# Two-layer attention and expert kernel: state products for two tiles in one run, two more residuals through TensorE, and a new written order

## The chip, the cores and the metric

The kernel runs on one core of a Trainium2 chip. The metric is the device time of one execution in microseconds. A profiled execution also gives a trace of every instruction on TensorE (PE, its weight loads PEld), VectorE (DVE), ScalarE (ACT), GpSimd (POOL) and SyncE (SP, which here only issues DMAs).

## What is computed

2048 tokens of width 576 pass through two layers. Each layer is a linear attention block with a residual, and then a block that picks one of 64 experts per head, with a residual. Cut to what matters:

```python
def _A_ref(x, wqkv, wo):                       # 32 heads of 18
    qkv = (x @ wqkv) ...
    phi = lambda t: jnp.where(t > 0, t + 1, jnp.exp(t)) + 1e-6
    pq, pk = phi(q), phi(k)
    kv = jnp.einsum("bhsd,bhse->bhde", pk, v)
    z = jnp.einsum("bhsd->bhd", pk)
    o = (pq @ kv) / (pq . z + 1e-6)
    return o @ wo
def _B_ref(x, w_q, k1, k2, u, v):              # 32 heads, 8 x 8 experts, one chosen
    q1, q2 = halves of x @ w_q
    s1, s2 = q1 @ k1.T, q2 @ k2.T
    e = argmax(s1) * 8 + argmax(s2)
    return sum over heads of gelu(x . u[e]) * v[e]
x = x + _A_ref(layernorm(x), wqkv, wo)
x = x + _B_ref(layernorm(x), w_q, k1, k2, u, v)   # and both once more
```

The state kv and its sum need all tokens of a layer. So each layer has a part that ends with the state, and a part that starts with it.

## The kernel before

The tokens stand in 16 tiles of 128. Every float32 matrix is split into a high and a low part, and a product of a tile with a 576 wide weight is 28 matmuls in groups of 10, 8 and 10 (high with high, high with low, low with high). These are the groups of lines L236 and L452 in the profile, 10 or 8 matmuls to a row.

The first part of a layer takes each tile through normalizing (yf), turning (by TensorE as ptf, or by a DMA through memory: t_df is written and rf is read back), splitting (thif and tlof), and the products for key, value and query (ppk, ppv, ppq). ScalarE and VectorE make the positive keys and queries (ek, eq) and copy the values into one of two buffers (v, L275). `front_state` (L320) then adds the tile's keys times values to the state kva, one accumulator in PSUM for the whole layer: ten matmuls that write 64 of 128 columns each. PSUM is a pool of four accumulators of 128 x 1024, and all results of TensorE go through it.

In layer 0 another job runs beside this: the experts' keys are multiplied into w_q (`fold_mm`, L618), 16 steps of 8 matmuls each that write 32 columns, from 64 loads of 288 KB on SyncE (fold). The loads land in a ring of ten buffers. Positive queries of layer 0 are stored (pq_d) and read back later.

The second part forms the state's sum and its product with wo (z, m), and takes each tile through the division (o), turning (pto, or t_do and ro), the output product ppo (L452), the residual x (L441, VectorE), normalizing (yb), turning (ptb, or t_db and rb), the scores pps (14 matmuls, L494), a choice of the best expert in code on VectorE for a group of two tiles, which ends with ct (L558), the gelu (g), and the product of both (cg, on GpSimd, L565). `exp_T` turns it on TensorE (pc, L473) and splits it on ScalarE and VectorE (chi, clo, L476 and L478), and `exp_out` multiplies it with the experts' values (po, L585, 4 matmuls, two with chi and two with clo) and adds the residual on VectorE (L441). For some tiles of layer 1 the residual goes another way: `exp_base` (L574) multiplies the tile's x with the identity matrix into the accumulator po first, 2 instructions that the trace shows as 4 records, the output is added to it there, and ScalarE copies the sum out (L590). Before the change these are tiles 10, 11 and 12. The last group of layer 1 is the tiles 8 and 9.

The order of all of it is written out by hand. Each step is a generator cut into pieces at its `yield`s, and a text lists the pieces: `st0.3` is the next piece of the state step of layer 0, tile 3, and `num1.0x2` two pieces of the division of tile 0 in layer 1. `play` runs them one by one, inside `with in_order(PE, ACT, DVE, POOL, SP)`, so every engine, SyncE's queue of DMAs with it, executes its instructions strictly in the order in which the text emits them. An instruction that waits holds back all that stands behind it on its engine. `wu` pieces are matmuls on scratch data at the start (warm_up).

The text's pieces that the change and the prediction touch: st (state), F and wf (fold matmuls and their loads), wk, wv, wq (weights), fl and ln (first tiles), bT (turning before the scores), po and base.

## Time and profile before

| | |
|---|---|
| median of 3 runs | 722.04 us (721.49 to 722.27) |
| profiled execution | 720.1 us |
| its span in the trace | 718.3 us, so 1.8 us lie outside |
| mean granted TensorE clock | 0.992 |
| PE busy | 694.6 us (97%) |
| DVE, ACT, POOL busy | 465.2, 340.0, 232.4 us |
| DMA moved | 131.23 MB, mean 183 GB/s |

In rows of the timeline the first number is the start in microseconds from the span's start, the second the duration from the first start to the last end of the instructions of the row. Then come the engine, the line, the operation, what it writes and reads, the shape, and how many. In square brackets stands the idle time of that engine just before the row, and what ended it. The ends of matmuls are modelled and overlap the next start by a little, so costs of TensorE are best taken from start to start.

The page's 40 slices of the span (busy tenths of TensorE and VectorE, granted TensorE clock, DMA):

```profile
PE   8999999999998999999999999999999999999994
...
DVE  6763713121437788779867857631477798898776
...
PEclk9999999999999999999999999999999999999996
DMA  8799789700128557574786586444568575545302
```

TensorE is the full row; VectorE is nearly full in the stretches around 260 to 400 and 560 to 700 us, where the second parts of the layers run.

### The profile page before, as it was taken

What the parts mean: (1) busy time and instruction counts of PE and PEld (TensorE: products, weight loads), DVE (VectorE), ACT (ScalarE), POOL (GpSimd) and SP (SyncE); (2) the same over time, 40 slices, a digit from 0 to 9 for tenths busy, and PEclk for the clock granted to TensorE, in tenths of its full rate; (3) what the DMA queues carried; (4) which work ended last, traced back from release to release, by engine and by line L of the source; (5) the groups of instructions that cost most, each with busy time, mean ns of one, the idle gap of its engine ahead of it and who ended that gap; (6) DMA issues with size and microseconds to landing.
All of it is one profiled execution on the core that took longest, in us unless ns stands there. A gap on an engine that the chain in (4) does not pass through costs nothing.

```text
span 718.3 us, 14467 instructions
## 1 busy us (share of the span) xinstructions
PE 694.6 (97%) x5292; PEld 640.5 (89%) x5292; DVE 465.2 (65%) x840; ACT 340.0 (47%) x645; POOL 232.4 (32%) x490
## 2 busy tenths in 40 slices
PE   8999999999998999999999999999999999999994
PEld 5998988999996988988999999999999899898873
DVE  6763713121437788779867857631477798898776
ACT  5552422211324446464755575564565645644342
POOL 4231100000032455445642622420135545444242
PEclk9999999999999999999999999999999999999996
DMA  8799789700128557574786586444568575545302
GB/s 268 228 315 321 221 280 291 237 18 1 34 75 251 189 168 238 186 242 133 238 266 214 175 253 199 144 153 103 162 182 243 185 198 177 163 158 182 100 16 99
DMA packets 109276, 131.23 MB, mean 183 GB/s; under 512 B 11926, under 2 KB 69270, under 8 KB 109206
## 3 DMA queue, kind: packets, MB, share of 16 engines
q1 hardware_dynamic: 109206, 130.32, 58.4%
q8 instruction: 41, 0.67, 0.4%
q14 instruction: 29, 0.24, 0.1%
HBM read 80.83 MB, written 49.45 MB: 181 GB/s over the span
## 4 chain that ended last, share of the span: by engine, by line
PE 51%; DVE 14%; issue 13%; DMA 10%; POOL 5%; ACT 3%; SPq 3%; POOLq 0%; DVEq 0%; ACTq 0%
PE ppk L236 10%; PE ppq L236 9%; PE ppv L236 9%; PE pps L494 8%; PE ppo L452 6%; DMA ro<-t_do 2%; PE fold_ps L618 2%; PE po L585 2%; SPq L218 2%; PE kva L320 2%; DVE x L441 1%; DVE m L527 1%; DMA rf<-t_df 1%; POOL o L418 1%; DMA whi<-hl_d 1%
## 5 line engine op out<-in xcount | busy, mean ns | idle before, releaser
L236 PE MATMUL ppk<-whi,thif 128*128 128x288 f32 x320 | 49.9, 300 | 2.8 <-ACT thif L224 1.4
L226 DVE TENSOR_TENSOR tlof<-rf,thif 128x640 fp32r<-128x640 f32 x27 | 22.2, 826 | 45.8 <-ACT thif L224 13.3
L452 PE MATMUL ppo<-ohi,thio 126*128 126x288 f32 (+1 forms) x320 | 49.9, 298 | 0.2
L236 PEld LDWEIGHTS ppk<-whi,thif 128*128 128x128 f32 x320 | 44.4, 188 | 5.6 <-ACT thif L224 1.9
L236 PE MATMUL ppk<-whi,tlof 128*128 128x288 f32 x320 | 48.4, 295 | 0.0
L236 PE MATMUL ppv<-whi,thif 128*128 128x252 f32 x320 | 48.2, 296 | 0.0
L236 PE MATMUL ppv<-whi,tlof 128*128 128x252 f32 x320 | 47.9, 295 | 0.0
L452 PEld LDWEIGHTS ppo<-ohi,thio 126*128 126x128 f32 (+1 forms) x320 | 44.5, 189 | 1.6 <-ACT thio L224 0.5
L236 PEld LDWEIGHTS ppv<-whi,thif 128*128 128x128 f32 x320 | 44.6, 189 | 0.7 <-DVE ek L252 0.2
L236 PEld LDWEIGHTS ppv<-whi,tlof 128*128 128x128 f32 x320 | 44.9, 189 | 0.0
L494 PE MATMUL pps<-shi,thib 128*128 128x512 f32 x160 | 43.4, 401 | 1.3 <-DVE x L441 0.8
L236 PEld LDWEIGHTS ppk<-whi,tlof 128*128 128x128 f32 x320 | 44.5, 188 | 0.0
L494 PE MATMUL pps<-shi,tlob 128*128 128x512 f32 x160 | 42.5, 395 | 0.6 <-DVE tlob L226 0.6
L275 ACT ACTIVATE v<-ppv 128x252 f32<-128x252 f32 x64 | 20.8, 379 | 45.9 <-PE ppv L236 27.7
L236 PE MATMUL ppk<-wlo,thif 128*128 128x288 f32 x256 | 39.8, 296 | 0.8 <-POOL wlo L131 0.8
L452 PE MATMUL ppo<-ohi,tloo 126*128 126x288 f32 x256 | 40.3, 295 | 0.1
L252 DVE SCALAR_TENSOR_TENSOR ek<-ppk,ek 128x576 f32<-128x576 f32 x32 | 24.2, 756 | 24.7 <-ACT ek L246 23.3
L452 PE MATMUL ppo<-olo,thio 126*128 126x288 f32 x256 | 40.1, 295 | 0.0
L236 PE MATMUL ppv<-wlo,thif 128*128 128x252 f32 (+1 forms) x256 | 39.3, 295 | 0.0
L170 ACT ACTIVATE yb<-x,mb 128x576 f32<-128x576 f32 x32 | 24.8, 774 | 30.5 <-POOL mb L167 27.8
L236 PE MATMUL ppq<-whi 128*128 128x288 f32 x260 | 39.0, 298 | 0.0
L184 ACT ACTIVATE yb<-x,rsb 128x640 f32<-128x640 f32 x32 | 29.4, 920 | 18.6 <-POOL rsb L175 17.8
(175 smaller groups left out, 1685.7 us busy)
## 6 DMA issues: line engine op xcount, KB each, us to landing
fold<-in_wq_t SPq DMA_DIRECT2D x64, 288.0 KB
t_df<-qf SPq DMA_DIRECT2D x27, 320.0 KB
rf<-t_df SPq DMA_DIRECT2D x108, 80.0 KB
t_do<-qo SPq DMA_DIRECT2D x27, 320.0 KB
ro<-t_do SPq DMA_DIRECT2D x108, 80.0 KB
whi<-hl_d SPq DMA_DIRECT2D x26, 320.0 KB
t_db<-qb SPq DMA_DIRECT2D x25, 320.0 KB
rb<-t_db SPq DMA_DIRECT2D x100, 80.0 KB
```

The lines of the kernel that those rows point to most:

```text
L170: nc.scalar.activation(y.rearrange("p a b -> p (a b)")[:, :D], xt, AF.Square, bias=m[:, 0:1], accum_out=m[:, 1:2])
L184: nc.scalar.activation(y, x2, AF.Identity, scale=rs[:, 0:1], bias=rs[:, 1:2])
L218: nc.sync.dma_start(r[32 * a:32 * a + 32].rearrange("r (i e) -> r i e", i=4), t_d[kind, t][:, a * w:(a + 1) * w].rearrange("(i r) e -> r i ...
L226: (nc.gpsimd if (who or kind, l) in LO_POOL or (who or kind, l, t) in LO_POOL else nc.vector).tensor_tensor(l4, src, h.bitcast(F32), op=AL ...
L236: nc.tensor.matmul(o[:, at:at + c1 - c0], tt[a == "lo"][:, b, :], wb[:, cols + c0:cols + c1], start=(i == 0), stop=(i == len(todo) - 1))
L252: nc.vector.scalar_tensor_tensor(e2, halves(p), 0.0, e2, op0=ALU.max, op1=ALU.add)
L275: nc.scalar.activation(vt[:, c:c + 2].rearrange("p c h e -> p (c h) e")[:, :, :63], x.rearrange("p (c e) -> p c e", c=4), AF.Copy)
L320: nc.tensor.matmul(a[64 * h:64 * h + 64, c * 72:c * 72 + n], vt[:, c, h], fk[:, k0:k0 + n], start=(t == 0 and c == 0), stop=(t == NT - 1), ...
L452: nc.tensor.matmul(p[:, h * 512:h * 512 + HALF], hl[a][:r, b], w[:r, h * HALF:(h + 1) * HALF], start=(i == 0), stop=(i == len(todo) - 1))
L494: nc.tensor.matmul(p[:, :512], hl[a == "lo"][:, b, :], shi[:, b] if w == "hi" else slo[:, blocks(REM)[b][1]], start=(i == 0), stop=(i == l ...
L585: nc.tensor.matmul(p[:, b * 512:b * 512 + HALF], c[i], vmix[:, b * HALF:(b + 1) * HALF], start=(i == 0 and not based), stop=(i == 1))
L618: nc.tensor.matmul(p[32 * j:32 * j + 32, at:at + c1 - c0], kpad[:, ch // 2, 24 - 8 * a:56 - 8 * a], st[:, c0:c1], start=(a == 0), stop=(a ...
```

## The change

`front_state` is called for every odd tile and does the ten matmuls of the tile before and of its own in one run; the accumulator of a layer's state is taken at tile 1, not 0. The score step is written a little differently, with the same instructions. Tiles 8 and 9 of layer 1 get their residuals through `exp_base` too (the set BASE is not read by the code; the pieces `base1.8` and `base1.9` in the text are what counts). The text is new from end to end. Warm-up matmuls are 29 and were 27.

```diff
-BASE = {10, 11, 12}
+BASE = {10, 11, 12, 8, 9}
...
     def front_state(l, t):
-        fk, vt = tt.pop(("fk", l, t)), v5[t % 2]
-        if t == 0:
+        if t == 1:
             kva[l] = psum(f"kva{l}")
         a = kva[l]
-
-        for c in range(NB):
-            for h in range(2):
-                k0, n = (c * HC + 54 * h, 72) if c < 4 else (4 * HC + 36 * h, 36)
-                nc.tensor.matmul(a[64 * h:64 * h + 64, c * 72:c * 72 + n], vt[:, c, h], fk[:, k0:k0 + n],
-                                 start=(t == 0 and c == 0), stop=(t == NT - 1), skip_group_check=True)
-
+        for u in (t - 1, t):
+            fk, vt = tt.pop(("fk", l, u)), v5[u % 2]
+            for c in range(NB):
+                for h in range(2):
+                    k0, n = (c * HC + 54 * h, 72) if c < 4 else (4 * HC + 36 * h, 36)
+                    nc.tensor.matmul(a[64 * h:64 * h + 64, c * 72:c * 72 + n], vt[:, c, h], fk[:, k0:k0 + n],
+                                     start=(u == 0 and c == 0), stop=(u == NT - 1), skip_group_check=True)
...
-            po1.12 po1.11 po1.12 po1.11 sel1.8 po1.12 sel1.8 gel1.8 sel1.8x2 po1.15x2 cT1.8x3 po1.8 po1.9 po1.8x2 po1.9x2
...
+            po1.11x2 sel1.8x5 po1.15x2 cT1.8x3 po1.9x3 po1.8x3
```

In the rows of the order below, a name's last number only tells buffers apart and the number before it is the tile.

**State runs, TensorE, first part of layer 1 (near 398 us in the trace before).** Before:

```order
L473 MATMUL pc_8_5081<-ident,cg_8_5069 128x128 x2
L320 MATMUL kva_3742<-ek_5_4778,v_1_87 64x72 x8
L320 MATMUL kva_3742<-ek_5_4778,v_1_87 64x36 x2
L320 MATMUL kva_3742<-ek_6_4926,v_0_86 64x72 x8
L320 MATMUL kva_3742<-ek_6_4926,v_0_86 64x36 x2
L585 MATMUL po_8_5114<-vmix,chi_8_5110 128x288 x2
L585 MATMUL po_8_5114<-vmix,clo_8_5111 128x288 x2
```

Now:

```order
L472 MATMUL pc_8_5069<-ident,cg_8_5060 128x128 x2
L320 MATMUL kva_4145<-ek_4_4617,v_0_86 64x72 x8
L320 MATMUL kva_4145<-ek_4_4617,v_0_86 64x36 x2
L320 MATMUL kva_4145<-ek_5_4803,v_1_87 64x72 x8
L320 MATMUL kva_4145<-ek_5_4803,v_1_87 64x36 x2
L583 MATMUL po_8_5111<-vmix,chi_8_5092 128x288 x2
L583 MATMUL po_8_5111<-vmix,clo_8_5093 128x288 x2
```

The run had the keys ek of tiles 5 and 6 and now has those of 4 and 5; tile 6's value product stands just ahead in both. Tile 4's own run, which stood alone elsewhere, is gone. Over both layers the state's 320 matmuls stood in 21 runs (12 of them of a single tile, one of four) and now stand in 16, each of two tiles.

**Normalizing of tile 0 in layer 1, ScalarE (near 560 us).** yb is made in two steps (L170, L184); thib_2 is a high part that comes back by DMA. Before:

```order
L244 ACTIVATE eq_4_7091<-ppq_4_7062 128x576
L245 ACTIVATE eq_4_7091<-eq_4_7091 128x576
L246 ACTIVATE eq_4_7091<-eq_4_7091,small 128x576
L224 ACTIVATE thib_2_7125<-rb_2_7015 128x640
L170 ACTIVATE yb_0_7168,mb_0_7157<-x_0_6996,mb_0_7157 128x576
L184 ACTIVATE yb_0_7168<-x_0_6996,rsb_0_7174 128x640
L170 ACTIVATE yb_1_7190,mb_1_7185<-x_1_7171,mb_1_7185 128x576
L200 ACTIVATE thib_0_7223<-ptb_0_7194 128x640
```

Now:

```order
L170 ACTIVATE yb_0_7091,mb_0_7001<-x_0_6998,mb_0_7001 128x576
L244 ACTIVATE eq_4_7093<-ppq_4_7062 128x576
L245 ACTIVATE eq_4_7093<-eq_4_7093 128x576
L246 ACTIVATE eq_4_7093<-eq_4_7093,small 128x576
L184 ACTIVATE yb_0_7091<-x_0_6998,rsb_0_7097 128x640
L224 ACTIVATE thib_2_7144<-rb_2_7057 128x640
L170 ACTIVATE yb_1_7153,mb_1_7151<-x_1_7141,mb_1_7151 128x576
L200 ACTIVATE thib_0_7192<-ptb_0_7135 128x640
```

Both of tile 0's steps moved ahead of thib_2, the first also ahead of query tile 4's finish. On TensorE the turning of tile 0 (ptb_0) moved from behind the output product of tile 13 to ahead of it.

**The end, TensorE.** po with x and ident is `exp_base`. Before:

```order
L473 MATMUL pc_11_8940<-ident,cg_11_8937 128x128 x2
L585 MATMUL po_11_8735<-vmix,chi_11_8947 128x288 x2
L585 MATMUL po_11_8735<-vmix,clo_11_8948 128x288 x2
L585 MATMUL po_12_8931<-vmix,chi_11_8947 128x288 x2
L585 MATMUL po_12_8931<-vmix,clo_11_8948 128x288 x2
L473 MATMUL pc_8_8991<-ident,cg_8_8985 128x128 x2
L585 MATMUL po_8_8998<-vmix,chi_8_8994 128x288 x2
L585 MATMUL po_8_8998<-vmix,clo_8_8995 128x288 x2
L585 MATMUL po_9_9003<-vmix,chi_8_8994 128x288 x2
L585 MATMUL po_9_9003<-vmix,clo_8_8995 128x288 x2
```

Now:

```order
L472 MATMUL pc_11_8938<-ident,cg_11_8934 128x128 x2
L583 MATMUL po_12_8921<-vmix,chi_11_8943 128x288 x2
L583 MATMUL po_12_8921<-vmix,clo_11_8944 128x288 x2
L572 MATMUL po_11_8960<-x_11_8513,ident 128x288 x2
L583 MATMUL po_11_8960<-vmix,chi_11_8943 128x288 x2
L583 MATMUL po_11_8960<-vmix,clo_11_8944 128x288 x2
L572 MATMUL po_8_8970<-x_8_8795,ident 128x288 x2
L472 MATMUL pc_8_8999<-ident,cg_8_8993 128x128 x2
L583 MATMUL po_9_8724<-vmix,chi_8_9002 128x288 x2
L583 MATMUL po_9_8724<-vmix,clo_8_9003 128x288 x2
L583 MATMUL po_8_8970<-vmix,chi_8_9002 128x288 x2
L583 MATMUL po_8_8970<-vmix,clo_8_9003 128x288 x2
```

Tile 11's identity product (before: earlier, behind the scores of tile 11) comes behind tile 12's output, and tile 8's ahead of the last pc; tile 9's took the place that tile 11's had. On VectorE the two residuals behind the last clo are gone, and on ScalarE two copies stand last.

Elsewhere: the 16 fold steps stand in 11 runs on TensorE and stood in 9. At the start, SyncE asks for the weight blocks 0, 1, 3, 2, 4 and for tile 2 between the last two, where it asked for 1, 0, 2, 3, 4 and tile 2 later; ScalarE rounds weight block 0 ahead of scaling tile 0, and GpSimd's small key step stands ahead of the first tile's statistics. Behind the first query products the value product of tile 2 stands where the key product of tile 2 stood. On SyncE the load for the last part of fold step 9 stands behind the store of query tile 3 and the four loads of tile 13's turned rows.

188 lines of the change are left out of this document (88 added, 100 removed).

## The prediction

> **What bounds the kernel now.** I read the busy line first, then windows of it, then TensorE's timeline for what ended each of its waits.
>
> ```profile
> PE 694.6 (97%) x5292; PEld 640.5 (89%) x5292; DVE 465.2 (65%) x840; ACT 340.0 (47%) x645; POOL 232.4 (32%) x490
> ```
>
> TensorE is busy for 694.6 of 718.3 us, and no other engine that computes is above 65%. So a new order can win in two ways only: TensorE's work gets shorter, or the 718.3 - 694.6 = 23.7 us in which it is not busy get fewer. The windows say where those are (columns: window, its length, then busy time and instructions of PE, PEld, DVE, ACT and POOL, then granted clock, DMA share and GB/s).
>
> ```profile
> 0.00:40.00 40.00, 35.42 (x253) 29.16 (x254) 29.26 (x59) 23.61 (x38) 15.62 (x41) 1.00 0.82 245
> 40.00:204.00 164.00, 164.00 (x1461) 155.46 (x1460) 57.62 (x108) 45.83 (x104) 9.10 (x23) 1.00 0.57 183
> 204.00:240.00 36.00, 34.17 (x312) 27.95 (x311) 20.57 (x40) 15.06 (x34) 12.08 (x24) 1.00 0.65 200
> ...
> 560.00:680.00 120.00, 117.33 (x744) 107.10 (x743) 103.97 (x191) 62.05 (x111) 57.42 (x114) 1.00 0.57 170
> ...
> 706.00:718.30 12.30, 3.12 (x12) 2.23 (x10) 6.05 (x16) 1.58 (x4) 1.13 (x2) 0.51 0.32 120
> ```
>
> The head lacks 4.6 us, the turn to the first output products 1.8, the last 12.3 us lack 9.2: together 15.6 of the 23.7. From 40 to 204 TensorE never stops; there only its own work counts. In 560 to 680 VectorE is busy for 104 of 120 us, so an order that makes VectorE late costs TensorE there.
>
> **The change part by part.** Durations are those of the profiled execution (720.1 us, span 718.3). The runs' median, 722.04, is 1.94 above it, and the sum is applied to both. A difference under 0.2%, 1.44 us, can't be told from none.
>
> *State products, two tiles in one run.* Each state run (kva, L320) writes 64-column pieces, and the products on both sides of it pay for the turn. TensorE's timeline (start, duration, engine, line, operation) has a run of two tiles and one of a single tile between like neighbours:
>
> ```profile
> 169.99 1.50 PE L236 MATMUL ppv<-whi,tlof 128*128 128x252 f32 x10
> 171.42 1.43 PE L320 MATMUL kva<-ek,v 128*64 128x72 f32 x40
> ...
> 174.25 1.22 PE L236 MATMUL ppk<-wlo,thif 128*128 128x288 f32 x8
> ...
> 176.64 1.50 PE L236 MATMUL ppk<-whi,thif 128*128 128x288 f32 x10
> 177.98 1.23 PE L236 MATMUL ppk<-wlo,thif 128*128 128x288 f32 x8
> 179.05 1.49 PE L236 MATMUL ppk<-whi,tlof 128*128 128x288 f32 x10
> 180.47 0.81 PE L320 MATMUL kva<-ek,v 128*64 128x72 f32 x20
> ...
> 182.63 1.23 PE L236 MATMUL ppk<-wlo,thif 128*128 128x288 f32 x8
> ```
>
> An undisturbed group of ten product matmuls takes 177.98 - 176.64 = 1.34 us. From 169.99 to 174.25 lie one such group, the run of two tiles, and one more group: the run costs 4.26 - 2.68 = 1.58. From 179.05 to 182.63 it is one tile between two groups: 3.58 - 2.68 = 0.90. Joining two singles is worth 2 x 0.90 - 1.58 = 0.22 us. The order of TensorE has 21 state runs before and 16 now: 5 x 0.22 = **-1.1 us**. Nothing hides it, as these runs stand where TensorE doesn't stop. Bounds: -0.6 (half of the joins had another disturbance beside them) and -1.4. The pair also adds a wait: there are two value buffers, so ScalarE can't copy the values of the pair's successor until the pair's run is through, and the key finishes queued behind that copy on ScalarE wait with it. As TensorE has a whole product (3.8 us from 176.64 to 180.47) between a pair and the next use of what these copies free, I count 0; where that cover is missing it costs about the 0.7 to 1.3 of the waits that end on ScalarE in the fences below.
>
> *Fold products* (32-column pieces, L618): the same 128 instructions, in 11 runs instead of 9. Rows of TensorE, and of SyncE's issues (SPq) in the same stretch:
>
> ```profile
> 54.98 2.19 PE L618 MATMUL fold_ps<-fold,kpad 128*32 128x320 f32 x32
> 57.10 1.60 PE L236 MATMUL ppk<-whi,thif 128*128 128x288 f32 x10
> 58.53 1.23 PE L236 MATMUL ppk<-wlo,thif 128*128 128x288 f32 x8
> ...
> 96.29 1.50 PE L236 MATMUL ppq<-whi,tlof 128*128 128x288 f32 x10
> ...
> 112.57 2.36 PE L618 MATMUL fold_ps<-fold,kpad 128*32 128x320 f32 x32
> ...
> 222.23 2.63 PE L618 MATMUL fold_ps<-fold,kpad 128*32 128x320 f32 x16
> ...
> 99.90 0.33 SPq L284 DMA_DIRECT2D pq_d<-eq  x1
> ...
> 108.32 2.47 SPq L218 DMA_DIRECT2D rf<-t_df  x4
> ```
>
> The group behind a run takes 58.53 - 57.10 = 1.43 instead of 1.34, and the run's start costs about as much: 0.1 to 0.25 us a run, two more runs, **+0.3**. A run can also wait inside for its loads: 2.36 instead of 2.19 at 112.57, and at 222.23 16 records took longer than 32. In the new order the last load for the fourth run of this kind (fold tile 9) stands on SyncE behind the store of query tile 3 and four loads of a turned tile. That store is issued 99.90 - (96.29 + 1.34) = 2.3 us after its product ends, the four loads take 2.5, and 288 KB need some 3 to 5 us to land (the last output, 715.15 to 718.3, is of that size and takes 3.1). So it lands 7.8 to 9.8 us after that product; TensorE reaches the matmul that needs it after two products (7.6) and the first fold tile (1.0), 8.6 us. Between 0 and 1.2: **+0.5**.
>
> *The head.* TensorE's waits there, and one rounding of a weight block on ScalarE:
>
> ```profile
> 11.41 0.54 PE L236 MATMUL ppk<-whi,thif 128*128 128x288 f32 x2 [0.41 <-DVE tlof L202]
> 14.93 0.54 PE L236 MATMUL ppk<-wlo,thif 128*128 128x288 f32 x2 [0.85 <-POOL wlo L131]
> 29.00 1.43 PE L320 MATMUL kva<-ek,v 128*64 128x72 f32 x40 [1.27 <-ACT v L275]
> 38.95 1.32 PE L236 MATMUL ppk<-whi,thif 128*128 128x288 f32 x8 [0.87 <-ACT thif L224]
> ...
> 9.15 0.68 ACT L128 ACTIVATE whi<-wst 128x576 fp32r<-128x576 f32 x1 [0.53 <-DMA wst<-in_wqkv]
> ```
>
> SyncE now asks for weight block 3 before block 2, and GpSimd clears its buffers later, so the matmul of 14.93 should find its low part. Tile 2 is asked for earlier, and a value product of tile 2 stands where the key product waited at 38.95. Against it: ScalarE rounds the first weight block ahead of scaling the first tile, which delays that tile by 0.68 and by the block's landing; GpSimd waits for a small key load ahead of the first tile's statistics; block 4 now follows tile 2 on the queue. Taking away 0.85 and 0.87 and paying 0.68 once gives **-1.0**; bounds -2.0 (nothing paid) and +1.0 (the delay paid twice, 0.85 and 0.87 kept in part). The wait of 29.00 stays: the same four products stand ahead of it.
>
> *Waits in the middle that the new order moves* (TensorE, then one row of ScalarE):
>
> ```profile
> 267.37 0.53 PE L585 MATMUL po<-vmix,chi 128*128 128x288 f32 x2 [0.47 <-ACT chi L476]
> ...
> 336.07 0.53 PE L585 MATMUL po<-vmix,chi 128*128 128x288 f32 x2 [0.41 <-DVE clo L478]
> 338.34 1.59 PE L236 MATMUL ppk<-whi,thif 128*128 128x288 f32 x10 [0.95 <-DVE x L441]
> ...
> 398.19 0.83 PE L320 MATMUL kva<-ek,v 128*64 128x72 f32 x20 [0.76 <-ACT v L275]
> ...
> 563.57 0.77 PE L196 MATMUL ptb<-ident,yb 128*128 128x128 f32 x5 [0.60 <-ACT yb L184]
> ...
> 559.53 0.74 ACT L224 ACTIVATE thib<-rb 128x640 fp32r<-128x640 f32 x1 [1.65 <-DVE eq L252]
> ```
>
> At 398 the state run waits for tile 6's values; now tiles 4 and 5 stand there, whose values were copied before: **-0.8**. At 338 a key product waits for a residual behind two output steps; now it stands between them: **-0.9** (0 if its accumulator comes free no sooner). At 563 TensorE waits for tile 0's normalized rows. ScalarE makes them behind the high part of tile 2 at 559.53, for which it stood idle for 1.65; now both of tile 0's steps come ahead of that. TensorE asks a product (3.8, 176.64 to 180.47) earlier. I take **-0.6**; if it is no sooner, TensorE waits up to 3.8 more. The other sign: ahead of the outputs of tiles 2 and 4 (the row of 336 is tile 4's) a state run stood between the transposed codes and the output that uses them, and covered ScalarE's and VectorE's halves. Now the output follows at once, as at 267, where 0.47 was idle. At 336 there were 0.41 anyway. So +0.5 and +0.1, **+0.6**, at most +1.2 if the low part is late by as much.
>
> *The last two tiles' residuals* (TensorE, VectorE, ScalarE at the end):
>
> ```profile
> 701.73 1.13 PE L574 MATMUL po<-x,ident 128*128 128x288 f32 x4
> ...
> 705.72 0.42 PE L585 MATMUL po<-vmix,clo 128*128 128x288 f32 x2
> 710.85 0.69 PE L473 MATMUL pc<-ident,cg 128*128 128x128 f32 x2 [4.70 <-POOL cg L565]
> 712.07 0.85 PE L585 MATMUL po<-vmix,chi 128*128 128x288 f32 x2 [0.53 <-ACT chi L476]
> ...
> 713.67 0.68 PE L585 MATMUL po<-vmix,clo 128*128 128x288 f32 x2
> ...
> 714.39 0.76 DVE L441 SCALAR_TENSOR_TENSOR x<-po,x 128x576 f32<-128x576 f32 x1
> ...
> 701.93 0.65 ACT L590 ACTIVATE x<-po 128x576 f32<-128x576 f32 x1
> ```
>
> Two more residuals enter the accumulator as identity products of about 1.1 us each. Tile 9's takes the place that tile 11's had. Tile 11's goes behind tile 12's output and tile 8's follows, both inside the 4.70 us; 4.70 - 2.2 = 2.5 us stay idle, and the code chain on VectorE that ends the wait is unchanged. Cost 0, or +2.2 if that cover were gone. Behind the last matmul a copy of 0.65 replaces a residual of 0.76: **-0.1**. Tile 9 holds one accumulator of four to the end, as tile 11 did nearly; I take 0, at most +0.7, the wait for one copy.
>
> The clock: the end runs at a granted 0.51 (last window), and 0.42 became 0.68 across the idle stretch. With 2.5 us idle instead of 4.70 the clock may stay up. The last eight rows' matmuls, 714.35 - 712.07 = 2.28 us, would take 2.28 x 0.42 / 0.68 = 1.4, and the transposition 0.26 less: up to -1.1. The longest idle stretch that left the clock at 1.00 is at most the 1.8 of the window from 204; between that and 4.70 the trace is silent, so this is a rival and not in the sum.
>
> The Trainium skill, page "TensorE: Matmul & The Clock Gate", Part 1, has the clock halve after an idle window of about 3.4 us that runs free. By that rule 2.5 us can't fill one and the sum would be the rival's. The trace agrees with its half clock (0.51).
>
> *The rest of the order.* The order of tasks on TensorE is nearly the same from 40 to 200 us and from 650 on, yet all engines' places shifted a little, and the traced order has waits of 0.4 to 0.95 us where two engines just miss (six in the rows above). I removed some by name; a new order will have its own. Bounds 0 and +3 (four of 0.75); I take two small ones, **+1.0**.
>
> Sum: -1.1 + 0.3 + 0.5 - 1.0 - 0.8 - 0.9 - 0.6 + 0.6 - 0.1 + 1.0 = **-2.1 us**: profiled execution 718.0, median 722.04 - 2.1 = **719.9**.
>
> **The rivals.** *(a) No change.* The joined runs save 1.1, the head pays for the earlier rounding what it saves, and the waits that I removed come back where TensorE asks sooner: -1.1 + 0.8 + 0 = -0.3, 721.7. For it: chains through VectorE in 560 to 680 don't get shorter by being asked for earlier. Against it: the wait at 398 ends by order alone.
>
> *(b) Slower: the turning of tile 0 near 563.* TensorE asks 3.8 us earlier for what came 0.60 late. If ScalarE's second step is as late as before, because the query's finishing steps that still stand ahead of it end no sooner, TensorE stands 0.6 + 3.8 = 4.4 us: +3.8 in place of -0.6, a sum of +2.3, 724.3. It decides from a wait of about 3.5 us, where the sum passes +1.44. Against it: ScalarE stood idle for 1.65 us just ahead of that step.
>
> *(c) The clock stays up at the end:* 719.9 - 1.1 = 718.8.
>
> *(d) The removed waits go and none come,* the head at its bound: without the +1.0 and the +0.5, head -2.0: 719.9 - 2.5 = 717.4.
>
> **How the numbers follow.** The forecast has a chance of 0.35, (a) 0.26, (b) with other late producers of its kind 0.19, (c) 0.12, (d) 0.08. The forecast's own range is 718.6 to 721.3. The range over all, 716.3 to 724.1, takes in (a), (c) and (d) and all of (b) but its upper part. Faster by over 0.2% (below 720.6): three quarters of the forecast's, all of (c)'s and (d)'s and some of (a)'s, 0.53; within (to 723.5) 0.27; slower 0.20.
>
> **What would show it.** Right: 16 state runs in the trace, all of two tiles; about 1 us less busy time of TensorE from 40 to 204; no wait before the state run near 398 or the key product near 338; less than 0.5 before tile 0's turning near 560; about 2.5 us idle ahead of the last transposition, two ScalarE copies last. Wrong: a key product that starts later than 11.9 with the stall behind it kept; waits over 1 us for normalized tiles or accumulators from 540 to 700; fold runs of 2.5 us or more between 60 and 130.

## The result: slower by 1.1%, outside the range

The changed kernel's median is 729.95 us over four runs (728.4 to 732.19), beside 722.15 for the kernel before: a ratio of 1.0111 [1.0091, 1.013]. The forecast was 719.9 (716.3 to 724.1). The sign is wrong, and the time lies above the range. In three of the kernels below, and once in the kernel before, a single execution took 1121 to 3519 us; these are left out of the medians and ratios here.

The profiled execution took 730.2 us with a span of 728.3, 10.0 more than before. Its busy line:

```profile
PE 699.2 (96%) x5302; PEld 643.8 (88%) x5302; DVE 467.5 (64%) x836; ACT 340.2 (47%) x647; POOL 230.7 (32%) x490
```

TensorE is busy for 4.6 us more and idle for 5.4 more (728.3 - 699.2 = 29.1, before 23.7). TensorE's timeline shows how the 10.0 grow. Both orders reach the product with `pick` (line 359 before, 358 now) once per layer, when the layer's state is complete; the two rows of before, and then those of the changed kernel:

```profile
209.51 1.16 PE L359 MATMUL z<-kvb,pick 128*128 128x126 f32 x8
...
513.06 1.05 PE L359 MATMUL z<-kvb,pick 128*128 128x126 f32 x8
```

```profile
212.51 1.16 PE L358 MATMUL z<-kvb,pick 128*128 128x126 f32 x8
...
520.00 1.05 PE L358 MATMUL z<-kvb,pick 128*128 128x126 f32 x8
```

It is 3.0 late at the first, 6.9 at the second and 10.0 at the end: in these two traces each third of the program loses 3 to 4 us, and there is no single culprit. TensorE's timeline of the changed kernel, with the waits of over 1 us (the 1.19 ahead of the first warm-up matmul left out, 1.17 before) and the two fold runs of 32 records that took longer than 2.18 (start, duration, engine, line, operation, and in brackets the wait ahead of it and what ended it):

```profile
51.93 1.60 PE L236 MATMUL ppv<-whi,thif 128*128 128x252 f32 x10 [3.02 <-DVE eq L252]
...
66.97 3.48 PE L616 MATMUL fold_ps<-fold,kpad 128*32 128x320 f32 x32
...
125.75 2.66 PE L616 MATMUL fold_ps<-fold,kpad 128*32 128x320 f32 x32
...
221.78 2.18 PE L377 MATMUL m<-wob,kvb 128*126 128x288 f32 x8 [2.22 <-POOL o L429]
...
340.05 0.53 PE L583 MATMUL po<-vmix,chi 128*128 128x288 f32 x2 [2.20 <-DVE clo L477]
...
387.04 1.60 PE L236 MATMUL ppk<-whi,tlof 128*128 128x288 f32 x10 [2.61 <-DVE tlof L226]
...
540.37 1.56 PE L236 MATMUL ppq<-whi 128*128 128x288 f32 x10 [1.03 <-DMA whi<-hl_d]
...
578.05 0.77 PE L196 MATMUL ptb<-ident,yb 128*128 128x128 f32 x5 [2.42 <-ACT yb L184]
...
721.36 0.44 PE L472 MATMUL pc<-ident,cg 128*128 128x128 f32 x2 [3.05 <-POOL cg L563]
```

The wait of 2.22 replaces one of 1.82 in the same place before, and the last one replaces the 4.70. At 340, 0.41 grew to 2.20. The other waits and the 1.30 us inside the run at 66.97 are new. Behind the two waits at 340 and 387 the clock adds its part (columns: window, length, busy time of PE, PEld, DVE, ACT and POOL, granted clock, DMA share, GB/s):

```profile
340.00:345.00 5.00, 4.95 (x26) 4.95 (x27) 4.69 (x10) 2.38 (x5) 2.53 (x8) 0.66 0.44 139
...
385.00:390.00 5.00, 2.96 (x14) 2.67 (x15) 3.06 (x5) 2.25 (x4) 0.23 (x1) 0.85 0.94 321
390.00:395.00 5.00, 5.00 (x19) 3.94 (x19) 2.20 (x4) 2.47 (x5) 0.50 (x1) 0.81 0.69 198
```

Twice 5 x (1 - 0.66) or 5 x 0.15 + 5 x 0.19 makes 1.70 us: after each of these two waits TensorE runs for 3.4 us at half its clock, and the two waits of 2.20 and 2.61 cost 3.9 and 4.3 so. (Not after each wait of this size: the last section.)

**What is late in each place.** The four large waits that are new or grew have one pattern: a short step that TensorE needs soon stands, in the new order, behind steps of other tiles that wait themselves or take long. VectorE ahead of 51.93, where eq belongs to query tile 1 and its finish frees the accumulator that the value product takes:

```profile
47.62 0.46 DVE L152 BATCH_NORM_STATS2 stf<-xf 128x6 f32<-128x288 f32 x1 [1.39 <-DMA xf<-in_x]
...
50.60 0.41 DVE L251 TENSOR_SCALAR eq<-eq 128x576 f32<-128x576 f32 x1
51.12 0.76 DVE L252 SCALAR_TENSOR_TENSOR eq<-ppq,eq 128x576 f32<-128x576 f32 x1
```

The finish of query 1 stands behind the statistics of other tiles, which wait for their loads. VectorE ahead of 340.05, where clo is the low half of the codes of tile 4, and the lines 532 to 539 are steps of the choice of experts for tile 6, which nobody needs yet:

```profile
337.85 0.82 DVE L532 SCALAR_TENSOR_TENSOR q<-m 128x512 bf16<-128x512 bf16 x1
...
339.45 0.21 DVE L539 SCALAR_TENSOR_TENSOR m<-m 128x64 bf16<-128x64 bf16 x1
339.58 0.41 DVE L477 TENSOR_TENSOR clo<-pc,chi 128x256 fp32r<-128x256 f32 x1
```

VectorE ahead of 387.04, where tlof is the low part of tile 6:

```profile
382.07 0.85 DVE L206 STREAM_TRANSPOSE qf<-yf 128x640 f32<-128x640 f32 x1 [3.27 <-DMA t_do<-qo]
...
385.43 0.85 DVE L206 STREAM_TRANSPOSE qo<-o 128x640 f32<-128x640 f32 x1 [0.40 <-POOL o L429]
386.20 0.78 DVE L226 TENSOR_TENSOR tlof<-rf,thif 128x640 fp32r<-128x640 f32 x1
```

Tile 7's turning (qf) waited 3.27 us for a store that still read its buffer; it and the division and turning of tile 15 stood ahead of tile 6's step. And ahead of 578.05, first SyncE's issues, then GpSimd, then ScalarE:

```profile
564.05 0.32 SPq L284 DMA_DIRECT2D pq_d<-eq  x1
...
570.16 0.38 SPq L405 DMA_DIRECT2D pq<-pq_d  x1
...
574.00 1.43 POOL L417 TENSOR_TENSOR o<-pq,zb 128x576 f32<-128x576 f32 x1 [3.56 <-DMA pq<-pq_d]
...
575.68 0.19 POOL L167 TENSOR_SCALAR mb<-sumx 128x1 f32<-128x1 f32 x1
...
577.08 1.97 ACT L184 ACTIVATE yb<-x,rsb 128x640 f32<-128x640 f32 x2 [0.30 <-POOL rsb L175]
```

Query tile 15 is stored at 564.05 and asked for again only at 570.16; GpSimd waits 3.56 us for it, and the statistics of tiles 1 and 13, which ScalarE and then TensorE need, stand behind it.

### The profile page after: what moved, and what is told of

The parts are those of the page before. It is cut to its first block, busy times and chain, and to the rows that moved or that the text cites. A ratio compares the mean times of both kernels' runs of the same rounds, so it can differ in the third digit from the quotient of the medians.

```text
span 728.3 us, 14494 instructions
## 1 busy us (share of the span) xinstructions
PE 699.2 (96%) x5302; PEld 643.8 (88%) x5302; DVE 467.5 (64%) x836; ACT 340.2 (47%) x647; POOL 230.7 (32%) x490
## 4 chain that ended last, share of the span: by engine, by line
PE 68%; DVE 12%; DMA 7%; POOL 3%; issue 3%; ACT 3%; SPq 3%; POOLq 0%; DVEq 0%; ACTq 0%
PE ppq L236 13%; PE ppv L236 13%; PE ppk L236 13%; PE ppo L451 11%; PE pps L492 8%; PE fold_ps L616 3%; PE kva L320 2%; PE po L583 2%; SPq L218 1%; PE m L377 1%; DVE m L525 1%; POOL o L417 1%; DMA rb<-t_db 1%; DMA wst<-in_wqkv 1%; DMA xf<-in_x 1%
## 5 line engine op out<-in xcount | busy, mean ns | idle before, releaser
L327 POOL MEMSET wob<- 128x576 f32 x10 | 5.4, 580 | 122.4 <-PE fold_ps L616 122.4
L170 ACT ACTIVATE yb<-x,mb 128x576 f32<-128x576 f32 x32 | 24.7, 772 | 32.0 <-POOL mb L167 31.7
L184 ACT ACTIVATE yb<-x,rsb 128x640 f32<-128x640 f32 x32 | 29.5, 920 | 19.8 <-POOL rsb L175 19.1
```

Of the source, the lines that this page charges most:

```text
L170: nc.scalar.activation(y.rearrange("p a b -> p (a b)")[:, :D], xt, AF.Square, bias=m[:, 0:1], accum_out=m[:, 1:2])
L184: nc.scalar.activation(y, x2, AF.Identity, scale=rs[:, 0:1], bias=rs[:, 1:2])
```

## The experiments

Two theories stood against each other. By the first, the named parts do about what the forecast has for them, and the new order of the other engines costs the time, at a few places that can be mended singly. By the rival, the joined state runs or the residuals through TensorE themselves cost it. In the edits a piece of the text is one step, and what was moved is marked with - and +.

**The two parts alone, in the old order.** First the residuals of tiles 8 and 9:

```diff
-O1.9x3 ldx1.8 base1.11 bT1.12
+O1.9x3 ldx1.8 base1.9 bT1.12
...
-po1.12 po1.11 po1.12 po1.11 sel1.8 po1.12 sel1.8 gel1.8 sel1.8x2 po1.15x2 cT1.8x3 po1.8 po1.9 po1.8x2 po1.9x2
+po1.12 base1.11 po1.12x2 po1.11 base1.8 po1.11x2 sel1.8x5 po1.15x2 cT1.8x3 po1.9x3 po1.8x3
```

> The kernel before, with one part of the change alone: tiles 8 and 9 of layer 1 get their residuals as identity products, and the order from the transposition of tile 10's codes to the end is that of the change. Theory 1 (the loss of the change is a few places of its new order where an in-order engine holds something that TensorE needs behind an instruction that waits; the parts themselves do what they were priced at): -0.1 for a copy in place of a residual behind the last matmul, and as between the two traces the last transposition, product and end come 0.2 to 0.7 us earlier relative to the matmuls ahead of them: 721.4 to 722.1, a ratio of 0.999 to 1.000. Theory 2 (the parts of the change cost time of their own; here the two identity products of 1.1 us each on the path and an accumulator held): +1 to +2.2, a ratio of 1.0014 to 1.003.

Measured: 722.41 us, 1.0004 [0.9989, 1.0018]. No difference, as forecast (0 and -0.1). The wait ahead of the last turning fell from 4.70 to

```profile
713.68 0.44 PE L473 MATMUL pc<-ident,cg 128*128 128x128 f32 x2 [3.05 <-POOL cg L565]
```

which is half a microsecond more than the 2.5 of the forecast, and the granted clock still falls to half there, 1.7 us behind the wait's end.

Then the joined state runs, with the pieces of the even tiles taken out of the old text and a few pieces near the pairs moved so that each pair has its keys and values:

```diff
-        fk, vt = tt.pop(("fk", l, t)), v5[t % 2]
-        if t == 0:
+        if t == 1:
...
+        for u in (t - 1, t):
+            fk, vt = tt.pop(("fk", l, u)), v5[u % 2]
...
-k0.4 v0.6 k0.4x2 st0.4 v0.6 F0.4 ... q0.4 st0.5 ln0.14x2 fT0.14 wf0.33 fT0.14 st0.6 F0.6
+k0.4 v0.6 k0.4x2 st0.5 v0.6 F0.4 ... q0.4 ln0.14x2 fT0.14 wf0.33 fT0.14 F0.6
```

> The kernel before, with the other part alone: the state products of two tiles in one run, at the place where the odd tile's products stood or behind the later tile's finished keys, 16 runs in place of 21; where a value copy would overwrite the buffer of a tile that is still to be added, it is put behind the run. Theory 1: five runs fewer at 0.22 us, -1.1 (bounds -0.6 and -1.4), 721.0, a ratio of 0.998 to 0.999, and at most one new wait of under 1 us. Theory 2 (two value buffers make ScalarE's copies, and the products that need the accumulators, wait for the pair): +2 or more, 724 and above, a ratio over 1.003, with TensorE waiting for copies of values (v) or for accumulators between 100 and 250 us.

Measured: 727.87 us, 1.0087 [1.0065, 1.011]: slower by 6. The joining does about what it was priced at: two of the pairs stand next to each other, so the trace has 15 state runs, six fewer, an estimate of 6 x 0.22 = 1.3 us, and TensorE's busy time falls by 1.2 us (694.6 before):

```profile
PE 693.4 (95%) x5292; PEld 640.0 (88%) x5292; DVE 467.2 (64%) x840; ACT 339.4 (47%) x645; POOL 233.1 (32%) x490
```

But in this order the pair's keys and values wait for each other. TensorE, and then ScalarE, near 180 us:

```profile
174.42 1.58 PE L236 MATMUL ppk<-whi,thif 128*128 128x288 f32 x10 [0.92 <-ACT v L277]
...
180.50 1.59 PE L236 MATMUL ppk<-whi,thif 128*128 128x288 f32 x10 [2.10 <-DVE ek L252]
```

```profile
184.99 0.65 ACT L275 ACTIVATE v<-ppv 128x252 f32<-128x252 f32 x2 [5.91 <-PE kva L320]
...
185.64 0.67 ACT L248 ACTIVATE ek<-ppk 128x576 f32<-128x576 f32 x1
```

Both value buffers are taken until the state run of tiles 10 and 11, which starts at 184.41, reads them. The values of tiles 12 and 13 were computed before and stay in two of the four accumulators until then: ScalarE stands for 5.91 us at their copies, which begin at 184.99. The state has the third accumulator. So each key product in between has only the fourth, and waits until the copy of tile 11's values (0.92) or the finish of the key product ahead of it (2.10) has emptied it. With a third one near 125 (1.26) they make 4.3 us between 60 and 204, where the order of before has no wait. The rival is half right: joined runs need an order made for them. The changed order has that, as TensorE's timeline shows no wait ahead of a row between 52 and 218 us.

**Each third alone.** Up to the z step of layer 0 both orders have run the same pieces, and nearly so up to that of layer 1. Each of three kernels takes one third from the new order and the rest from the old; runs of one tile or two follow each layer's order.

```diff
-[before: start ... zs0.0) [before: zs0.0 ... zs1.0) [before: zs1.0 ... end]
+[after:  start ... zs0.0) [before ...             ) [before ...           ]   first third
+[before ...             ) [after:  zs0.0 ... zs1.0) [before ...           ]   middle third
+[before ...             ) [before ...             ) [after:  zs1.0 ... end]   last third
```

> The two orders have run exactly the same pieces when layer 0's state sum z begins (209 us in the trace before) and nearly the same when layer 1's begins (513 us), so the program can be cut there and put together from the old and the new order. Here the first part (to layer 0's z) has the new order with joined state runs, the rest is the kernel before. Between the two traces z of layer 0 starts 3.0 us later in the change. Theory 1 (each part's own late inputs cost what its trace shows, and the parts add): +3.0, 724.8, a ratio of 1.0042. Theory 3 (a delay is taken back where the next engine was late anyway, so the parts don't add): +0 to +1.5, a ratio under 1.002.

> The old order up to layer 0's z and from layer 1's z on, the new order with joined state runs of layer 1 between them. From z to z the change is 6.9 - 3.0 = 3.9 us longer in its trace; the waits of 2.20 at 340 and 2.61 at 387 with 2.9 us of slow clock behind them lie here. Theory 1: +3.9, 725.7, a ratio of 1.0054. Theory 3: under +2, or much more than +3.9 where the first part's delay had given the other engines time.

> The kernel before up to layer 1's z, then the new order, with the five residuals through identity products. From layer 1's z to the end the change is 10.0 - 6.9 = 3.1 us longer in its trace, with the wait of 2.42 at 578; the end itself (the residuals) was worth nothing that could be measured when done alone. Theory 1: +3.1, 724.9, a ratio of 1.0043. Theory 3: +0 to +1.5.

Measured: 724.38, 1.0036 [1.0016, 1.0055]; 723.64, 1.0034 [1.0009, 1.0059]; 723.53, 1.0036 [1.0019, 1.0053]. The three make 1.0106, and the whole change 1.0111: each third costs about 2.5 us, and within the intervals they add up. The first keeps the new head, which is faster, and still loses. In the middle third the waits before the state run at 398 and the key product at 338 are gone as forecast, and the new ones outweigh them.

**The middle third: two steps on VectorE.** The wait at 340, put into the kernel before: tile 4's low half of the codes goes behind four of tile 6's steps.

```diff
-cT0.4 gel0.6 st1.1 cT0.4x2 v1.3 st1.2 sel0.6 oT0.11
+cT0.4 gel0.6 st1.1 cT0.4 sel0.6 cT0.4 v1.3 st1.2 oT0.11
```

> The kernel before with one step moved: the low part of tile 4's codes on VectorE stands behind four of tile 6's choice steps, as in the change. These take 1.6 us there, so TensorE's wait of 0.41 at 336 becomes about 2.0, and by the trace of the change the granted clock falls behind it for some 1.4 us more. Theory 1: +1.6 to +3.0, a ratio of 1.002 to 1.004. Theory 3: the later waits on VectorE at 338 (0.95) and on ScalarE at 398 (0.76) take most of it back: under +0.8, a ratio under 1.001.

Measured: 722.96, 1.002 [1.0004, 1.0035]. TensorE's row and the window behind it:

```profile
339.37 0.85 PE L585 MATMUL po<-vmix,chi 128*128 128x288 f32 x2 [2.26 <-DVE clo L478]
```

```profile
339.00:344.00 5.00, 4.63 (x22) 4.38 (x23) 3.48 (x9) 1.74 (x4) 1.56 (x5) 0.66 0.27 75
```

One piece moved makes the wait of 2.26 and the half clock in the old order, and the wait of 0.95 behind it goes. The cause of the wait at 340 is shown. Its price by the ratio is 1.4 us (0.3 to 2.5 by the interval).

The reverse, in the changed kernel:

```diff
-gel0.6x2 sel0.6 cT0.4x2 gel0.6 cT0.4 gel0.6 po0.4
+gel0.6x2 cT0.4x2 gel0.6 cT0.4 sel0.6 gel0.6 po0.4
```

> The changed kernel with one of the six alone: the low part of tile 4's codes on VectorE stands ahead of tile 6's choice steps. Theory 1: the wait of 2.20 us at 340 becomes about 0.4 to 0.7, as in the kernel before at 336, and the granted clock stays at 1.00 behind it (1.4 us): -2.9 to -3.6, 726.4 to 727.1. Theory 3: the 340 wait goes, and the next one, 2.61 us at 387, grows by what was won, or the choice of tile 6 comes later and TensorE waits for it: 729 to 730.

Measured: 730.82, 1.0129 [1.0107, 1.0152]: no gain. At 340 0.93 is left and the clock stays up, but the time moved on:

```profile
351.09 0.81 PE L320 MATMUL kva<-ek,v 128*64 128x72 f32 x20 [0.85 <-DVE ek L252]
...
389.07 1.27 PE L236 MATMUL ppk<-whi,tlof 128*128 128x288 f32 x5 [3.48 <-DVE tlof L226]
```

TensorE came to tile 6's low part earlier, and waited there longer. So the step at 387 should be the one that sets the time of this stretch. Tile 6's two steps, ahead of tile 7's turning:

```diff
-po0.7x2 fT1.7x2 num0.15x5 oT0.15x2 fT1.6x2 k1.6
+po0.7x2 fT1.6x2 fT1.7x2 num0.15x5 oT0.15x2 k1.6
```

> The changed kernel with one step moved: in the run with six places the wait at 387 had not gone, and the names of the order, counted through, show why: the low part that TensorE waits for there is tile 6's, not tile 5's, so the wrong step had been moved. Here tile 6's high and low part stand ahead of tile 7's turning on VectorE, which waits 3.27 us for a buffer that a late store still reads. Theory 1: the wait of 2.61 us at 387 and the slow clock behind it (1.5) go: -2.6 to -4.1, a ratio to the kernel before of 1.0055 to 1.0075 instead of 1.0111. Theory 3: 1.010 to 1.012, with the wait at the next place that needs VectorE.

Measured: 726.85, 1.0046 [1.003, 1.0062]. From 1.0111, these two steps are worth 4.7 us, which is the wait of 2.61 and the half clock behind it (1.70) within the intervals. Both edits on the kernel with the new middle third alone:

> The kernel before with the new order from z to z (measured 1.0034), and in it the two steps mended: the low part of tile 4's codes and tile 6's low part. The waits there are 2.19 at 337.8 and 1.54 at 383.0. Theory 1: -1.3 and -1.5, a ratio of 0.9985 to 1.0005. Theory 3: 1.002 to 1.0035.

Measured: 722.01, 0.9999 [0.9981, 1.0017], from 1.0034. Within the intervals, these steps on VectorE cost all that the middle third lost. What it gained by order (0.76 and 0.95) is used up by what is left at the places of 340 and 351, 0.93 and 0.84 in this trace.

**The first third: a wait that moved into the fold runs.** The finish of query 1 ahead of three tiles' statistics, on the kernel with the new first third:

```diff
-ln0.10x3 fl0.4 ln0.4x2 ... ln0.15x2 q0.0 fT0.3x2 ... wf0.2 q0.1 fT0.15 fl0.9 ln0.9 fl0.7 ln0.7 fT0.4 q0.1
+ln0.10x3 q0.1 fl0.4 ln0.4x2 ... ln0.15x2 q0.0 q0.1 fT0.3x2 ... wf0.2 fT0.15 fl0.9 ln0.9 fl0.7 ln0.7 fT0.4
```

> The kernel before with the new order up to layer 0's z (measured 1.0036), and in it query tile 1's finish ahead of three tiles' statistics. In that kernel's trace the wait there was 0.94 (3.02 in the change's), and the second fold run waited inside for its loads (3.90 us instead of 2.18), which stays. Theory 1: -0.9 to -1.5, a ratio of 1.0015 to 1.0025, the rest being the fold run's 1.7 us. Theory 3: 1.003 or more, since the fold run waits for its loads the longer the sooner TensorE comes.

Measured: 725.27, 1.0043 [1.0028, 1.0058], beside 1.0036 without the edit. The wait at 51 is gone and nothing is gained. The second fold run shows why. Its rows in the kernel with the new first third, in this one, and in one with the edits of all three thirds, which is told below:

```profile
65.74 3.90 PE L616 MATMUL fold_ps<-fold,kpad 128*32 128x320 f32 x32
```

```profile
68.26 1.16 PE L616 MATMUL fold_ps<-fold,kpad 128*32 128x320 f32 x4 [0.33 <-DMA fold<-in_wq_t]
```

```profile
64.97 4.09 PE L616 MATMUL fold_ps<-fold,kpad 128*32 128x320 f32 x32
```

Whenever it was started, it ended 8.7 to 9.3 us after the end of the first fold run: 70.45 after 61.77 in the changed kernel, and in these three 69.64 after 60.54, 69.42 after 60.10, 69.06 after 59.77 (8.6 to 9.4 in all seven traces in which it waits). Only the first run frees the buffers that the second run's last six loads go into. SyncE's issues in the changed kernel, where the first run starts at 59.59:

```profile
60.78 2.70 SPq L606 DMA_DIRECT2D fold<-in_wq_t  x6
```

In the order of before the second run starts 8.5 us behind the end of the first and ends 10.7 behind it, with no wait. So a product of query 2 was put between the two runs, and one of query 5 behind:

```diff
-wf0.17 F0.2 wf0.18 wf0.19 F0.3 wf0.20 wf0.21 wf0.22 wf0.23 q0.2 wf0.24 Fo0.0 fT0.8 FT0.0 q0.2 ... q0.5x4 FT0.0x2
+wf0.17 q0.2 F0.2 wf0.18 wf0.19 F0.3 wf0.20 wf0.21 wf0.22 wf0.23 wf0.24 q0.2 Fo0.0 q0.2 fT0.8 ... q0.5 FT0.0 q0.5x3 FT0.0x2
```

> The kernel before with the new order up to layer 0's z; query tile 1's finish moved as in first_eq1 (1.0043), and query tile 2's product and finish moved ahead of the second fold run, query tile 5's product behind it. In four kernels that run ended 8.7 to 9.3 us after the first run's end, whenever it began (64.97 to 66.97): its loads go into the buffers that the first run frees. With a product more between them TensorE comes 11 us behind and need not wait. Theory of the ring: the run takes 2.2 instead of 3.9 to 4.1, -1.7 to -1.9, and with the wait at 51.9 gone too a ratio of 0.9995 to 1.0020. If VectorE or ScalarE's lateness is what bounds the first third: 1.003 or more, with a new wait of 2 us behind the fold's transposition.

Measured: 723.1, 1.0017 [0.9999, 1.0035]. The second run takes its 2.18 again:

```profile
70.29 2.18 PE L616 MATMUL fold_ps<-fold,kpad 128*32 128x320 f32 x32
```

From 1.0043 to 1.0017, the median gains about what the run had lost. So by the medians the fold run was the larger part of what the first third lost. Its trace alone doesn't show that: z of layer 0 comes at 211.58, beside 211.53 without the edit, with a wait of 1.32 at 55.24 and a later fold run of 3.03. The wait ahead of the two runs was hidden by them at least in part. It also differs from one execution to the next: in the five traces with the new first third unedited it is 0.94 (the new first third alone), 1.13, 1.87, 2.32 and 3.02 (the profile of the whole change, with statistics that wait for loads ahead of it).

**The last third: not settled.** Tile 15's query asked for right behind its store, in the changed kernel:

```diff
-q1.15 num1.6 oT1.6 bT1.2 lq1.4 ... oT1.14 ldq1.15 num1.15x2
+q1.15 ldq1.15 num1.6 oT1.6 bT1.2 lq1.4 ... oT1.14 num1.15x2
```

> The changed kernel with one load moved: tile 15's stored query is read back right behind its store, as in the kernel before, and not behind eight loads of turned tiles and one of x. In the run with six places only the statistics behind it had been moved, and the 2.42 us came back as 3.14 at the next tile, whose turned rows hang on the same load. Theory 1 (the late load is the root): GpSimd's division of tile 15 no longer waits 3.56 us, TensorE's wait at 578 goes and none over 1 us follows up to 600: -2.4, a ratio of 1.0075 to 1.009. Theory 3: 1.010 to 1.012.

Measured: 729.83, 1.0101 [1.0055, 1.0146]: no gain. SyncE's issues:

```profile
567.87 0.32 SPq L284 DMA_DIRECT2D pq_d<-eq  x1
571.85 0.32 SPq L405 DMA_DIRECT2D pq<-pq_d  x1
572.26 1.81 SPq L218 DMA_DIRECT2D rb<-t_db  x4
```

The load's issue waits until the store is through, 3.98 us from issue to issue, and holds the four loads of tile 2's turned rows behind it. The wait at 578 went, and waits of 1.07 and 1.49 for tiles' high parts and normalized rows came.

Next, the statistics of tiles 1 and 13 ahead of tile 15's division, and a product of m ahead of the late query load, on the kernel with the new last third:

```diff
-num1.1 lq1.5 q1.14 num1.1 q1.14 num1.1 q1.14 oT1.13 M1.0 lq1.5
+num1.1 M1.0 lq1.5 q1.14 num1.1 q1.14 num1.1 q1.14 oT1.13 lq1.5
...
-oT1.14 ldq1.15 num1.15x2 num1.4 oT1.6 rl1.10 oT1.6 ldx1.3 O1.13x2 O1.1x2 ldx1.4 O1.13x2
+oT1.14 ldq1.15 O1.1x2 O1.13x4 num1.15x2 num1.4 oT1.6 rl1.10 oT1.6 ldx1.3 ldx1.4
```

> The kernel before with the new order from layer 1's z on (measured 1.0036), and in it two places mended: on GpSimd and ScalarE the statistics of tiles 1 and 13 both stand ahead of tile 15's division, which waits for a load (with tile 1's alone, or with the load moved, the wait came back at the next tile); and a product of the state's sum stands between a load and the query product that waits for it. The waits there are 1.70 at 569.4 and 1.22 at 532.4. Theory 1: -1.7 and -0.5 to -1.2, a ratio of 0.9995 to 1.0010. Theory 3: 1.002 or more, with the waits at the next tile.

Measured: 726.45, 1.0064 [1.0051, 1.0078]: slower than the 1.0036 without the edits. The wait at 569 is gone and a longer one stands at the scores of the next tile. TensorE, and then ScalarE:

```profile
584.13 2.30 PE L492 MATMUL pps<-shi,thib 128*128 128x512 f32 x5 [3.21 <-ACT thib L224]
```

```profile
583.35 0.74 ACT L224 ACTIVATE thib<-rb 128x640 fp32r<-128x640 f32 x1 [1.52 <-DMA rb<-t_db]
```

ScalarE's step ahead of it waits for a load of turned rows. So the loads of tile 2's turned rows were put ahead of the store of query tile 15 and its load right behind the store, with the product of m moved as before and the statistics left in place:

```diff
-q1.15 num1.6 q1.15 num1.6 oT1.6 bT1.2 lq1.4 ... oT1.14 ldq1.15 num1.15x2
+q1.15 num1.6 bT1.2 q1.15 ldq1.15 num1.6 oT1.6 lq1.4 ... oT1.14 num1.15x2
```

> The kernel before with the new order from layer 1's z on (1.0036); on SyncE's queue the four loads of tile 2's turned rows stand ahead of the store of query tile 15, and its load back right behind that store, as in the kernel before; and a product of the state's sum stands ahead of the query product that waits for a load. GpSimd's order is left as it is. If the late load is the cause: GpSimd's division of tile 15 runs 2 to 3 us sooner, TensorE's wait of 1.70 at 569 falls to 0.4 to 0.9 and none over 1 us follows up to 585, with the other place -1.3 to -2.0: a ratio of 1.0008 to 1.0018. If GpSimd's order by itself is: 1.003 or more.

Measured: 725.16, 1.0058 [1.0033, 1.0082], far from what was expected. The wait at 569 shrank to 0.63, and at the next tile's scores one is left:

```profile
583.66 1.44 PE L492 MATMUL pps<-shi,thib 128*128 128x512 f32 x5 [1.35 <-ACT thib L224]
```

By the medians, neither the held statistics nor the late load alone is the cause of what the last third loses. The trace is a little kinder. It came to z of layer 1 some 3 us late, though its order up to there is nearly that of before (1.70 of it is half clock behind a wait of 1.82 at 218.38), but from there to its end it takes 206.9 us, beside 207.4 with the new last third unedited, 209.7 with the statistics moved, and 204.8 to 206.5 in the eight traces with the old last third. What stays open is which step sets the end between 560 and 600 us.

**Several edits at once.** Six at once in the changed kernel came early in the study: the finish of query 1, query 2 ahead of the second fold run, tile 4's codes, the product of m, the statistics of tile 1, and low parts near 387. The last was the wrong tile: tile 5's steps were moved, and the key product there is tile 6's. The expectation names the wrong one too.

> The changed kernel with six places of its order mended, nothing else: query tile 1's positive part is finished ahead of three tiles' statistics (wait of 3.02 us at 51.9); query tile 2's product stands ahead of the fold run that waited inside for its loads (3.27 instead of 2.18 at 67.0); the low part of tile 4's codes stands ahead of tile 6's choice steps (2.20 at 340.05, with 1.4 us more at a granted 0.66 behind it); tile 5's low part stands ahead of the turning of tile 6 that waits for a DMA (2.61 at 387.0, with 1.5 at 0.81 to 0.85 behind it); a product of the state's sum stands between a load and the query product that waits for it (1.03 at 540.4); tile 1's statistics stand ahead of tile 15's division that waits for a load (2.42 at 578.05). Theory 1: the sum of the six with the slow clock behind two of them, 3.0 + 1.1 + 3.6 + 4.1 + 0.5 + 2.4 = 14.7, 730 - 14.7 = 715.3; some of it comes back as smaller waits, so 715 to 719, faster than before. Theory 3 (the waits move on: the engines off the path are late by themselves, so TensorE only stops somewhere else): 725 to 730. Theory 2: not below 722.

Measured: 731.97, 1.0143 [1.0099, 1.0186]. The wait at 390 stayed (2.94), and one of 3.14 for a high part came at 593.80, of the kind seen near 584 above.

Then five: query 1's finish, the queries around the second fold run, tile 4's codes, tile 6's steps, and the load of query 15 right behind its store.

> The changed kernel with five places mended: query tile 1's finish ahead of three tiles' statistics (51.9); query tile 2's product ahead of the second fold run and query tile 5's ahead of the fold's transposition, so that both the loads and the copy keep a product as cover (67.0); the low part of tile 4's codes (340); tile 6's low part (387); tile 15's load (578). Theory 1: by the lags that single steps left in the run with six places and by the waits, 2.0 + 1.1 + 1.8 + 4.1 + 2.4 = 11.4 us less than the change, 718.6, a ratio of 0.994 to 1.000. Half of it would be 1.003. Theory 3: 1.008 or more.

Measured: 725.52, 1.0043 [1.003, 1.0057]: 4.9 us better than the change and 7 short of the expectation. A wait of 2.22 for a finish on VectorE came at 77.37 behind the second fold run, and 0.90, 1.48 and 0.59 stand in 567 to 584.

And the edits of the three thirds together (query 1's finish, tile 4's codes, tile 6's steps, statistics and m product), once with the new head, once with the old first third:

> The changed kernel with all that has been found: query tile 1's finish, the low part of tile 4's codes, tile 6's low part, the statistics of tiles 1 and 13, the product ahead of the late query. Theory 1 (the parts add): 1.002 from the first part, 1.000 from the middle, 1.000 to 1.001 from the last: a ratio of 1.001 to 1.003. Theory 3: 1.004 or more, as with the five places of the earlier run.

> The old order up to layer 0's z, the new and mended one behind it: the middle third was measured at 0.9999 so mended, the last should be 0.9995 to 1.001. Theory 1: 0.9985 to 1.001; a version that is faster than the kernel before would be at the low end. Theory 3: 1.003 or more.

Measured: 727.37, 1.0072 [1.0054, 1.009], and 723.48, 1.0032 [1.0018, 1.0047]. Both have the late high part near 584 (2.38 and 2.43). The first also has the second fold run of 4.09 above. The edit of the queries around the fold runs is not in them, since it was found later. No kernel of the study beats the one before; the best stand at 0.9999 (the middle third mended) and 1.0004 (the residuals alone). The mended first and middle thirds together, with the old last third, were not run.

## Why the prediction was wrong, by its steps

The step that failed is **"the rest of the order"**: two small waits, +1.0, with bounds of 0 and +3 (four of 0.75). The new waits that the sum did not name are 3.02 at 51.93, 1.30 in the fold run, 2.61 at 387, 1.03 at 540 and 2.42 at 578, and +1.8 at 340, together 12.2, with 3.4 of half clock behind two of them. With the named gains, -3.1, that would be +12.5. The head gained 1.5 instead of 1.0 (1.7 by the start of the first query product, of which 0.7 is lost inside it, and 0.5 at the key product). Small waits of before that no term named went as well, 1.5 in all (0.52 at 315.82, and 0.36, 0.21 and 0.42 from 567 to 628), and small ones came, 1.7 in all (0.57 at 247.26, 0.69 at 406.43, and 0.40 more at 222). That makes 12.2 for the 10.0 measured. Two single traces don't agree better than by some 2 or 3 us: from z to z, the old order of the middle third takes 303.6 to 306.7 us in the eight traces that have it, and the trace of before is the shortest of them. So the list names the places, and their prices are those of one execution; the experiments price them at about 2.5 us a third, and the medians of the two kernels differ by 7.8.

The bound was wrong in its making. I took the size of a new wait from the waits of the order of before, 0.4 to 0.95. Those are what is left where an order has been fitted until engines just miss. A new order's misses have the length of what stands ahead of the late step: four choice steps (1.7), a wait for a load or a store (3.3 to 3.6). Such lengths stood in the trace of before as idle times of VectorE, ScalarE and GpSimd, and I had not looked for steps that moved behind them. Nor had I put in that a wait can cost the clock as well, though the end of the span showed it.

The other steps:

- *State products, -1.1.* Right: -1.2 of busy time in the old order with pairs alone, six runs fewer. "I count 0" for the two value buffers was right for the order of the change, which has no wait from 52 to 218, and wrong as a property of the joining: in the old order it costs waits of 0.92, 1.26 and 2.10, and some 6 us in all. The price named for the missing cover, 0.7 to 1.3, was too small.
- *Fold products, +0.3 and +0.5.* The late load for fold step 9 came as worked out: 2.66 at 125.75, 0.48 over an undisturbed run of 2.18. That it came so close is partly luck, as the ten traces with this run have 2.18 to 3.03 for it, 2.41 in the mean. What I had not seen is the second fold run, whose loads wait for the first run's buffers: +1.30.
- *The head, -1.0.* The stall of 14.93 went, and 0.87 before the key product became 0.39. A wait of 0.87 for the first tile's rows at 9.00 is new, near the 0.68 put down for the earlier rounding. But 3.02 came 10 us behind the key product. From the median of the first third alone nothing of the head is left to see.
- *At 398, -0.8, and at 338, -0.9.* Both waits are gone. Right.
- *At 563, -0.6.* Tile 0's rows were turned without a wait, so rival (b), the wait of 4.4 there, did not come. One of its kind did at the next tile: 2.42 at 578 for tile 1. The mechanism of (b) was right, its place was not: the statistics on GpSimd, not the finish on ScalarE, were late.
- *Cover of tiles 2 and 4, +0.6.* Tile 2's output waits 0.47 as worked out. Tile 4's waits 2.20 where 0.5 was expected, for another reason: four choice steps of tile 6 stand ahead of its low half.
- *The last two residuals, 0 and -0.1.* Right: 1.0004 alone. The idle time ahead of the last turning is 3.05, not 2.5, and rival (c), the clock that stays up, did not come: the kernel with the residuals alone is no faster.

Of the 3.1 that the named terms gain, the joins, 398 and 338 (2.8) came in full, and so did the tail's nothing. They are paid back several times over by waits that no term named.

## What to carry to other kernels

Where a change replaces a whole written order, the waits of the old order say nothing about the size of the new ones. For every engine, list the steps that TensorE waits for within the next few products, and look at what now stands ahead of each in its queue: a step that waits for a transfer, or several us of work that nobody needs yet, is the size of the wait to come. And a mended wait is worth its time only if no later step on the same stretch was hidden by it: here mending the second cause (at 387) was worth 4.7 us and mending the first alone (at 340) nothing.
